# Block inverse read along rows, and padded loads, in a chunked recurrence on one Trainium2 core

## The chip, the core and the metric

The kernel runs on one core of a Trainium2 chip. The engines are named as the profile names them: PE multiplies matrices (PEld loads its weights), DVE works on vectors, ACT is the scalar engine, POOL is GpSimd, and SP issues most of the DMA transfers. Each engine takes its own instructions in order. The metric is the time of one execution in microseconds, the median over runs. Three runs of the kernel before gave 1887.94, 1891.57 and 1893.30 us.

## The reference

Per batch (4) and head (8) a 40 x 40 state is carried over 768 steps; then all outputs go through a mixture of 8 experts whose gate is normalized in rows and columns.

```python
for t in range(S):
    y[:, :, t] = np.einsum('bhd,bhde->bhe', rt, state)
    Sa = np.einsum('bhde,bhe->bhd', state, at)
    state_decay = state * wt[:, :, None, :] - np.einsum('bhd,bhe->bhde', Sa, bt)
    state = state_decay + np.einsum('bhd,bhe->bhde', vt, kt)
# x: the outputs, (3072, 320)
P = np.exp(x @ w_gate - max)       # then 8 rounds of row and column normalization
for e in range(E):
    out += P[:, e:e + 1] * (np.maximum(x @ w1[e], 0.0) @ w2[e])
```

## The kernel before, in words

The 768 steps are cut into 12 chunks of 64. Within a chunk the recurrence becomes matrix products and one triangular system per head, whose inverse is formed explicitly. Four steps `b` (the batches) stand for each chunk `c`; four pairs of heads lie side by side in a tile.

`prep(c, b)` loads the inputs (`inp`, 522 KB), scans the decays on DVE (`q`, `g`), forms `kb` and `ab` on POOL, and multiplies to the triangular matrices `ll`, whose lower part goes out to DRAM (`ld`). Two chunks form a group; there are six groups. When a group's eight preparations are out, `load_lu` brings their 32 x 32 blocks back as `lu`, one small matrix a partition (128 partitions: 2 chunks, 2 blocks, 4 batches, 8 heads), by eight DMAs.

The inverse of all 128 blocks then runs on DVE alone, in `un`. `inv_diag` (steps 1 to 7) inverts the 8 x 8 diagonal blocks, column by column. `inv_off` fills the blocks beside the diagonal, first 8 x 8, then 16 x 16, each by two products of small matrices. Such a product is a `contract`: one multiplication that spreads all products into `pr` and one reduction over the innermost index. The second factor `m` is a block of `lu` or `un` read down its columns:

```python
in1=m.rearrange("u k r -> u r k").unsqueeze(1).broadcast_to([nu, n_c, n_r, n_k])
```

A row is 32 floats, so neighbours in a column lie 128 bytes apart. The largest product has 2048 terms a partition. `finish` transposes the whole inverse (1024 elements, into `tn`, which shares the memory of `pr`) and stores both forms to DRAM (`ud`, `nd`). `tload` loads them back in other layouts (`td`, `tt`), and `tmat` joins 32 x 32 blocks to 64 x 64 with two PE products (`gp`, `op`).

`recur(c, b)` is the recurrence itself. It loads `vz` (value rows into columns 0 to 63 of a 104-wide tile; the state `z` goes to columns 64 to 103 by two ACT copies at the end of the step before), `rb`, and the transposed values into `f`, and then alternates between engines: `av` (PE), `f` (DVE), `xc` (PE), `x`, `c` (ACT), `pu` (PE, with `tt`), `pm` (DVE), `c` (PE), `ws` (DVE), `y`, `z` (POOL), `zt` (PE), `vz` (ACT). Four of these chains are in flight, one per batch.

The list `ev` holds all calls with a time each, sorted; a scheduler then sets the order on every engine from that list and its own estimates. The order in the built program is what each engine follows. The last part of the kernel, the experts (lines 545 to 687), begins as soon as the first outputs are there and is not touched.

## Time and profile before

| | |
|---|---|
| Median of 3 runs | 1891.57 us |
| Profiled execution | 1888.5 us, span 1886.7 us, granted PE clock 0.945 |
| Busy over the span: PE, DVE, ACT, POOL | 1768.5, 1395.1, 853.9, 896.9 us |
| First 118 us: PE, DVE, POOL busy | 53.0, 83.9, 71.4 us |
| 118 to 560 us: PE, DVE, POOL busy | 403.5, 322.4, 216.1 us |
| DMA busy share in slices 1 to 12 of 40, tenths | 8 5 6 7 7 7 7 8 5 5 7 3 |

The profile is of one execution by the hardware profiler. Busy times count overlapping work on different engines twice, so they do not add up to the span. The chain of work that ended last is followed backwards from the last instruction through whatever released each step; only time on it shortens the run directly. The first 560 us hold the recurrence, the rest is the experts, during which PE is busy nearly all the time.

### The profile page before, as it was taken

Reading aid. Unit: us, or ns where it says so; the run is one execution under the profiler, and the core shown is the slowest. Engines: PE = TensorE matmul, PEld = TensorE weight load, DVE = VectorE, ACT = ScalarE, POOL = GpSimd, SP = SyncE. Lnnn points to the kernel's source line nnn. Section 1 sums busy time; section 2 is a strip of 40 time slices with the busy share of each in tenths; the row PEclk is TensorE's granted clock in tenths of the full one; section 3 lists DMA queues with packets and bytes.
Section 4 is the critical chain, followed back from the end, with each engine's and each line's share of the span. In section 5 each row is a group of like instructions: output and inputs, shape, how many; then the busy total and the mean of one; then the engine's idle time right before and its main releaser. Section 6 shows DMA issues by size and latency. Waiting matters only on the chain.

```text
span 1886.7 us, 31821 instructions
## 1 busy us (share of the span) xinstructions
PE 1768.5 (94%) x12035; PEld 1731.1 (92%) x12035; DVE 1395.1 (74%) x2330; ACT 853.9 (45%) x1845; POOL 896.9 (48%) x845
## 2 busy tenths in 40 slices
PE   4478989889998999999999999999999999999999
PEld 4368878789888999999999999999999999999999
DVE  7766768686579877776867777886776767777676
ACT  6346566655553444343433434345343433434342
POOL 6636457562345355371835628004461826537170
PEclk9568889988889999999999999999999999999999
DMA  8567777855732011110201102111110201111011
GB/s 192 102 131 160 137 156 144 176 128 102 164 96 70 32 43 37 37 61 14 73 26 49 55 19 74 55 33 38 37 55 19 73 19 56 37 37 57 17 37 42
DMA packets 187838, 136.26 MB, mean 72 GB/s; under 512 B 155941, under 2 KB 165285, under 8 KB 187685
## 3 DMA queue, kind: packets, MB, share of 16 engines
q1 hardware_dynamic: 184485, 128.98, 27.6%
q10 hardware_dynamic: 3200, 5.25, 1.1%
q8 instruction: 95, 1.56, 0.3%
q14 instruction: 58, 0.48, 0.1%
HBM read 113.74 MB, written 20.45 MB: 71 GB/s over the span
## 4 chain that ended last, share of the span: by engine, by line
PE 76%; DVE 10%; DMA 6%; issue 3%; POOL 2%; ACT 2%; SPq 1%; DVEq 0%; POOLq 0%; ACTq 0%
PE op L610 35%; PE p L545 32%; DMA inp<-in_inp_dram 2%; PE xc L259 2%; DVE pr L179 2%; PE pu L270 1%; PE av L251 1%; PE c L277 1%; DVE q L114 1%; PE ll L145 1%; PE lp L307 1%; PE gp L226 1%; DMA nd<-pr 1%; POOL ab L140 1%; DVE g L122 1%
## 5 line engine op out<-in xcount | busy, mean ns | idle before, releaser
L545 PE MATMUL p<-xch,wh 128*128 128x384 f32 (+1 forms) x1792 | 605.3, 339 | 5.2 <-DVE cs L654 1.8
L566 ACT ACTIVATE hh<-sm 128x384 fp32r<-128x384 f32 x512 | 269.5, 527 | 726.3 <-DVE sm L563 726.3
L610 PE MATMUL op<-wh,hh 128*128 128x320 f32 x1536 | 477.3, 311 | 1.0 <-ACT hh L566 0.9
L610 PE MATMUL op<-wl,hh 128*128 128x320 f32 x1536 | 474.7, 310 | 0.0
L610 PE MATMUL op<-wh,hl 128*128 128x320 f32 x1536 | 468.0, 310 | 4.4 <-DVE hl L569 4.4
L491 POOL TENSOR_TENSOR wl<-ws,wh 128x640 fp32r<-128x640 f32 x60 | 103.1, 1719 | 608.4 <-ACT wh L489 608.1
L569 DVE SCALAR_TENSOR_TENSOR hl<-sm,hh 128x384 fp32r<-128x384 f32 x512 | 370.8, 757 | 2.8 <-ACT hh L566 2.3
L545 PEld LDWEIGHTS p<-xch,wh 128*128 128x128 f32 (+1 forms) x1792 | 337.9, 189 | 8.4 <-DVE u L563 2.7
L545 PE MATMUL p<-xcl,wh 128*128 128x384 f32 x896 | 303.1, 338 | 0.0
L545 PE MATMUL p<-xch,wl 128*128 128x384 f32 x896 | 302.3, 337 | 0.0
L610 PEld LDWEIGHTS op<-wh,hh 128*128 128x128 f32 x1536 | 290.6, 189 | 1.7 <-ACT hh L566 1.5
L610 PEld LDWEIGHTS op<-wh,hl 128*128 128x128 f32 x1536 | 287.1, 188 | 5.4 <-DVE hl L569 5.3
L610 PEld LDWEIGHTS op<-wl,hh 128*128 128x128 f32 x1536 | 291.4, 190 | 0.0
L563 DVE TENSOR_TENSOR sm<-p,u 128x384 f32<-128x384 f32 x384 | 232.6, 615 | 9.2 <-PE p L545 0.4
L545 PEld LDWEIGHTS p<-xcl,wh 128*128 128x128 f32 x896 | 169.0, 189 | 0.0
L545 PEld LDWEIGHTS p<-xch,wl 128*128 128x128 f32 x896 | 169.0, 189 | 0.0
L563 DVE TENSOR_TENSOR sm<-p,p 128x384 f32<-128x384 f32 x128 | 71.3, 557 | 130.1 <-PE p L545 76.2
L563 DVE TENSOR_TENSOR p<-p,p 128x384 f32<-128x384 f32 x128 | 71.1, 555 | 101.5 <-PE p L545 101.0
L563 DVE TENSOR_TENSOR u<-p,p 128x384 f32<-128x384 f32 x128 | 70.8, 553 | 59.4 <-PE p L545 58.1
L145 PE MATMUL ll<-ab,kb 104*128 104x128 f32 x336 | 61.3, 340 | 50.6 <-POOL ab L140 22.2
L499 POOL TENSOR_TENSOR wl<-ss,wh 128x512 fp32r<-128x512 f32 x60 | 90.7, 1512 | 32.1 <-ACT wh L496 28.0
L145 PEld LDWEIGHTS ll<-ab,kb 104*128 104x128 f32 x336 | 53.2, 241 | 54.7 <-POOL ab L140 27.4
(161 smaller groups left out, 2845.0 us busy)
## 6 DMA issues: line engine op xcount, KB each, us to landing
ws<-in_wts_dram SPq DMA_DIRECT2D x60, 832.0 KB
inp<-in_inp_dram SPq DMA_DIRECT2D x42, 521.6 KB
rb<-in_r_dram SPq DMA_DIRECT2D x48, 208.0 KB
ld<-lt ACTq DMA_DIRECT2D x40, 128.0 KB
vz<-in_v_dram SPq DMA_DIRECT2D x48, 104.0 KB
f<-in_vt_dram SPq DMA_DIRECT2D x48, 80.0 KB
xd<-y SPq DMA_DIRECT2D x96, 40.0 KB
st<-in_inp_dram SPq DMA_DIRECT2D x6, 521.6 KB
```

What stands on the lines that cost most here:

```text
L114: nc.vector.tensor_tensor_scan(out=q.rearrange("r p t -> r (p t)"), data0=w65[:, 0:260], data1=one65, initial=0.0, op0=ALU.mult, op1=ALU.add)
L122: nc.vector.tensor_tensor_scan(out=g.rearrange("r p t -> r (p t)"), data0=w65[:, 260:516], data1=g1.rearrange("r p t -> r (p t)"), initial ...
L145: nc.tensor.matmul(ll[:, p], lhsT=kb[:, p], rhs=ab[:, p], start=True, stop=True)
L179: nc.vector.tensor_tensor(out=prv, in0=a.unsqueeze(2).broadcast_to([nu, n_c, n_r, n_k]), in1=m.rearrange("u k r -> u r k").unsqueeze(1).br ...
L259: nc.tensor.matmul(xc[h][:, p], lhsT=pp["sx"][:, p, h], rhs=f[:, p, h], start=True, stop=True)
L491: g.tensor_tensor(out=wl[:, 0:640], in0=raw[:, 256:896], in1=wh[:, 0:640], op=ALU.subtract)
L499: g.tensor_tensor(out=lv[:, 3:7], in0=so[:, :, 0], in1=hv[:, 3:7, 0], op=ALU.subtract)
L545: nc.tensor.matmul(o, lhsT=w_, rhs=x_, start=(j == 0), stop=(j == 3))
L563: eng.tensor_tensor(out=out, in0=x, in1=y, op=ALU.add)
L566: nc.scalar.activation(out=hh[:, f, h], in_=sm[f][:, h], func=AF.Relu)
L569: v.scalar_tensor_tensor(out=hl[:, f, h], in0=sm[f][:, h], scalar=0.0, in1=hh[:, f, h], op0=ALU.max, op1=ALU.subtract)
L610: nc.tensor.matmul(ops[i], lhsT=a[:, h, cs], rhs=w_[:, cw], start=(f == 0 and h == 0 and j == 0), stop=(last and h == 1 and j == 2))
```

## The change

The second factor of every contraction is now read along rows, from a transposed copy. `flip_l` writes the transposes of the blocks of `lu` that are needed into `lu`'s unused lower half, once a group, before the first elimination step. `flip_d` and `flip_h` write transposes of the finished diagonal blocks of `un` into a tile `tn` of its own. `inv_off` is replaced by `inv_8` and `inv_16`, in which no product has more than 1024 terms: the two of 2048 become two each. `finish` transposes only the last 16 x 16 block, the others being in `tn` already.

Apart from that, the host pads the value rows to the full 104 columns with zeros and the transposed values to 104 columns a head, so that both are loaded in one contiguous piece a partition (104 pieces of 1664 bytes instead of 416 of 256; 64 of 3328 instead of 512 of 160). Because the load of `vz` now overwrites the columns of `z`, it is issued one chunk ahead, in the step that precedes its use, and the first four are issued before any preparation. `vz` is no longer cleared at the start; `tn` is, on POOL.

```diff
-    prf = inv.tile([128, 2048], F32, name="pr")
+    prf = inv.tile([128, 1024], F32, name="pr")
+    tnf = inv.tile([128, 1056], F32, name="tn")
...
+        nc.gpsimd.memset(tnf, 0.0)
-        for t in vz_b + c1_b + lg_b:
+        for t in c1_b + lg_b:
...
     def contract(us, dst, a, m):
-        n_c, n_r, n_k = a.shape[1], m.shape[2], a.shape[2]
+        n_c, n_r, n_k = a.shape[1], m.shape[1], a.shape[2]
-            in1=m.rearrange("u k r -> u r k").unsqueeze(1).broadcast_to([nu, n_c, n_r, n_k]), op=ALU.mult)
+            in1=m.unsqueeze(1).broadcast_to([nu, n_c, n_r, n_k]), op=ALU.mult)
...
+    def flip_l(us):
+        lh = half_t(luf, us)
+        nc.vector.tensor_copy(out=lh[:, :, 8:16, 0:8], in_=lh[:, :, 0:8, 8:16].rearrange("u b k r -> u b r k"))
+        nc.vector.tensor_copy(out=lu[us, 16:32, 0:16], in_=lu[us, 0:16, 16:32].rearrange("u k r -> u r k"))
+    def flip_d(us):
+        nc.vector.tensor_copy(out=tnd[us, :, 0:8, 0:8], in_=und[us, :, 0:8, 0:8].rearrange("u b c j -> u b j c"))
+    def flip_h(us):
+        nc.vector.tensor_copy(out=half_t(tnf, us)[:, :, 8:16, 0:8],
+                              in_=half_t(unf, us)[:, :, 0:8, 8:16].rearrange("u b c j -> u b j c"))
...
+    def inv_8(us, i):
+        o, g, un_ = 16 * i, gt(us, 8), un[us]
+        contract(us, g, un_[:, o:o + 8, o:o + 8], lu[us, o + 8:o + 16, o:o + 8])
+        contract(us, un_[:, o:o + 8, o + 8:o + 16], g, tn[us, o + 8:o + 16, o + 8:o + 16])
+    def inv_16(us, i):
+        g, un_, tn_, l16 = gt(us, 16), un[us], tn[us], lu[us, 16:32, 0:16]
+        if i == 0:
+            contract(us, g[:, 0:8, 0:8], un_[:, 0:8, 0:16], l16[:, 0:8])
+            contract(us, g[:, 0:8, 8:16], un_[:, 0:8, 0:16], l16[:, 8:16])
+        elif i == 1:
+            contract(us, g[:, 8:16], un_[:, 8:16, 8:16], l16[:, :, 8:16])
+            contract(us, un_[:, 0:16, 16:24], g[:, :, 0:8], tn_[:, 16:24, 16:24])
+        else:
+            contract(us, un_[:, 0:8, 24:32], g[:, 0:8], tn_[:, 24:32, 16:32])
+            contract(us, un_[:, 8:16, 24:32], g[:, 8:16], tn_[:, 24:32, 16:32])
-    INV = [(inv_diag, (i,)) for i in range(1, 8)] + [(inv_off, a) for a in ((0, 8, 8), (16, 8, 8), (0, 16, 8))]
+    INV = [(flip_l, ())] + [(inv_diag, (i,)) for i in range(1, 8)] + [(flip_d, ())]
+    INV += [(inv_8, (0,)), (inv_8, (1,)), (flip_h, ()), (inv_16, (0,)), (inv_16, (1,)), (inv_16, (2,))]
...
     def recur(c, b):
-        nc.sync.dma_start(out=vz[:, :, 0:64], in_=d["v"][c, b])
+        if c + 1 < NCH:
+            vn = rot("vz", vz_b)
+            nc.sync.dma_start(out=vn, in_=d["v"][c + 1, b])
...
-        nc.sync.dma_start(out=f[0:64].rearrange("s p h x -> s (p h) x")[:, :, 64:104],
-                          in_=d["vt"][c, b].rearrange("s (g x) -> s g x", x=40))
+        nc.sync.dma_start(out=f[0:64].rearrange("s p h x -> s (p h x)"), in_=d["vt"][c, b])
...
-        vz = rot("vz", vz_b)
+        vz = vn
...
+    for b in range(NB):
+        nc.sync.dma_start(out=vz_cur[b], in_=d["v"][0, b])
...
     def finish(s, us):
-        nc.vector.tensor_copy(out=tn[us], in_=un[us].rearrange("u c s -> u s c"))
+        nc.vector.tensor_copy(out=tn[us, 16:32, 0:16], in_=un[us, 0:16, 16:32].rearrange("u c j -> u j c"))
```

The instructions' order moves with it. Lines of the changed kernel are 6 to 30 higher; 120, 128 and 161 are what 114, 122 and 155 were (scans `q`, `g` and the masked triangle), 185 and 188 are the contraction's multiplication and reduction (179 and 182 before). In the rows below a tile's number is its buffer.

DVE at the start, the preparations of the first group. Before, the first step of the recurrence (`f`) stands behind the fourth preparation:

```order
L114 SCALAR_TENSOR_TENSOR q<-st_189,cst 104x260
L118 RECIPROCAL g_196<-q 104x4
L122 SCALAR_TENSOR_TENSOR g_163<-st_189,g_196 104x256
L155 TENSOR_TENSOR sx_153<-ll,cst 64x8x64
L139 TENSOR_TENSOR ab_195<-st_189,g_163 40x4x64
L140 TENSOR_TENSOR ab_195<-st_189,g_163 40x4x64
L252 TENSOR_TENSOR f<-av,cst 104x8x64
L114 SCALAR_TENSOR_TENSOR q<-inp,cst 104x260
L118 RECIPROCAL g_196<-q 104x4
```
Now it stands behind the fifth:

```order
L120 SCALAR_TENSOR_TENSOR q<-inp,cst 104x260
L124 RECIPROCAL g_196<-q 104x4
L128 SCALAR_TENSOR_TENSOR g_167<-inp,g_196 104x256
L161 TENSOR_TENSOR sx_157<-ll,cst 64x8x64
L145 TENSOR_TENSOR ab_194<-inp,g_167 40x4x64
L146 TENSOR_TENSOR ab_194<-inp,g_167 40x4x64
L280 TENSOR_TENSOR f<-av,cst 104x8x64
L120 SCALAR_TENSOR_TENSOR q<-inp,cst 104x260
L124 RECIPROCAL g_196<-q 104x4
```
One preparation has moved ahead of `f`, which waits for `av`.

DVE at the end of the first group's inverse, from the last but one product to the finishing copy, before:

```order
L122 SCALAR_TENSOR_TENSOR st_146<-inp,g_196 104x256
L179 TENSOR_TENSOR pr<-gt,un 128x1024
L155 TENSOR_TENSOR st_189<-ll,cst 64x8x64
L182 TENSOR_REDUCE un<-pr 128x16x8
L114 SCALAR_TENSOR_TENSOR q<-inp,cst 104x260
L179 TENSOR_TENSOR pr<-gt,un 128x2048
L118 RECIPROCAL g_196<-q 104x4
L155 TENSOR_TENSOR st_146<-ll,cst 64x8x64
L182 TENSOR_REDUCE un<-pr 128x16x8
L122 SCALAR_TENSOR_TENSOR st_147<-inp,g_196 104x256
L114 SCALAR_TENSOR_TENSOR q<-inp,cst 104x260
```
and now:

```order
L124 RECIPROCAL g_196<-q 104x4
L185 TENSOR_TENSOR pr<-gt,tn 128x1024
L128 SCALAR_TENSOR_TENSOR st_147<-inp,g_196 104x256
L161 TENSOR_TENSOR st_146<-ll,cst 64x8x64
L188 TENSOR_REDUCE un<-pr 128x8x8
L120 SCALAR_TENSOR_TENSOR q<-inp,cst 104x260
L185 TENSOR_TENSOR pr<-gt,tn 128x1024
L124 RECIPROCAL g_196<-q 104x4
L188 TENSOR_REDUCE un<-pr 128x8x8
L128 SCALAR_TENSOR_TENSOR st_148<-inp,g_196 104x256
L161 TENSOR_TENSOR st_147<-ll,cst 64x8x64
```
The product of 2048 has become two of 1024 with a reduction of its own each, scans and triangles of the next preparations stand between them, and the finishing copy has shrunk.

DVE behind the third group's finishing copy, before:

```order
L331 COPY pr<-un 128x1024
L252 TENSOR_TENSOR f<-av,cst 104x8x64
L118 RECIPROCAL g_196<-q 104x4
L279 TENSOR_TENSOR ws<-c_2466,c_202 104x416
L272 TENSOR_TENSOR pm<-pu,cst 128x416
L122 SCALAR_TENSOR_TENSOR st_146<-inp,g_196 104x256
L155 TENSOR_TENSOR st_189<-ll,cst 64x8x64
L252 TENSOR_TENSOR f<-av,cst 104x8x64
L279 TENSOR_TENSOR ws<-c_2600,c_203 104x416
L155 TENSOR_TENSOR st_146<-ll,cst 64x8x64
L312 COPY lg<-lp 64x8 x2
```
and now:

```order
L361 COPY tn<-un 128x16x16
L192 COPY lu<-lu 128x2x8x8
L193 COPY lu<-lu 128x16x16
L176 TENSOR_TENSOR pr<-un,lu 128x4
L179 TENSOR_REDUCE un<-pr 128x4
L176 TENSOR_TENSOR pr<-un,lu 128x16
L179 TENSOR_REDUCE un<-pr 128x4x2
L176 TENSOR_TENSOR pr<-un,lu 128x36
L340 COPY lg<-lp 64x8
L179 TENSOR_REDUCE un<-pr 128x4x3
```
Before, the recurrence's `f`, `ws` and `pm` and the triangles followed, and the next group's first elimination step stood nineteen rows below the copy; now the flip of the next group's `lu` follows at once. On SP at the same place, from the loads of the first chunk's inverse on, before:

```order
L334 DMA nd<-pr 64x1024 x2
L213 DMA td<-ud 32x16x32 x2
L211 DMA td<-nd 32x16x32 x2
L217 DMA tt_190<-ud 32x16x32 x4
L285 DMA xd<-y 40x4x64 x2
L109 DMA inp<-in_inp_dram 104x1284 x2
L240 DMA rb<-in_r_dram 104x512
L242 DMA f<-in_vt_dram 64x8x40
L217 DMA tt_191<-ud 32x16x32
L285 DMA xd<-y 40x4x64 x2
L217 DMA tt_191<-ud 32x16x32 x3
L342 DMA lu<-ld 16x32x32 x4
```
and now:

```order
L363 DMA ud<-un 64x1024
L364 DMA nd<-tn 64x1024
L240 DMA td<-ud 32x16x32
L238 DMA td<-nd 32x16x32 x2
L240 DMA td<-ud 32x16x32
L244 DMA tt_190<-ud 32x16x32 x4
L372 DMA lu<-ld 16x32x32 x4
L244 DMA tt_191<-ud 32x16x32 x4
```
The last four loads of `lu` have moved from behind the second chunk's `tt` to ahead of it.

More of the change, by code (lines that the diff above doesn't have):

```diff
@@ L72, in attention, with half_t @@
     luf = inv.tile([128, 1056], F32, name="lu")
-    prf = inv.tile([128, 2048], F32, name="pr")
+    prf = inv.tile([128, 1024], F32, name="pr")
     gtf = inv.tile([128, 256], F32, name="gt")
-    un, lu, tn = (t[:, 0:1024].rearrange("u (a b) -> u a b", b=32) for t in (unf, luf, prf))
-    und, lud = (t.rearrange("u (b x) -> u b x", x=264)[:, :, 0:256].rearrange("u b (c j) -> u b c j", j=32)
-                for t in (unf, luf))
+    tnf = inv.tile([128, 1056], F32, name="tn")
+    un, lu, tn = (t[:, 0:1024].rearrange("u (a b) -> u a b", b=32) for t in (unf, luf, tnf))
+    und, lud, tnd = (t.rearrange("u (b x) -> u b x", x=264)[:, :, 0:256].rearrange("u b (c j) -> u b c j", j=32)
+                     for t in (unf, luf, tnf))
+    def half_t(t, us):
+        return t[us].rearrange("u (b x) -> u b x", x=528)[:, :, 0:512].rearrange("u b (c j) -> u b c j", j=32)
     for t in g1_b + ab_b:
@@ L180, in contract @@
             out=prv, in0=a.unsqueeze(2).broadcast_to([nu, n_c, n_r, n_k]),
-            in1=m.rearrange("u k r -> u r k").unsqueeze(1).broadcast_to([nu, n_c, n_r, n_k]), op=ALU.mult)
+            in1=m.unsqueeze(1).broadcast_to([nu, n_c, n_r, n_k]), op=ALU.mult)
         nc.vector.tensor_reduce(out=dst, in_=prv, op=ALU.add, axis=AX.X)
-    def inv_off(us, o, n, h):
-        gt = gtf[us, 0:n * n].rearrange("u (c r) -> u c r", r=n)
-        un_, lu_ = un[us], lu[us]
-        if h == n:
-            contract(us, gt, un_[:, o:o + n, o:o + n], lu_[:, o:o + n, o + n:o + 2 * n])
-            contract(us, un_[:, o:o + n, o + n:o + 2 * n], gt, un_[:, o + n:o + 2 * n, o + n:o + 2 * n])
-            return
-        contract(us, gt[:, 0:h], un_[:, o:o + h, o:o + n], lu_[:, o:o + n, o + n:o + 2 * n])
-        contract(us, gt[:, h:n], un_[:, o + h:o + n, o + h:o + n], lu_[:, o + h:o + n, o + n:o + 2 * n])
-        contract(us, un_[:, o:o + n, o + n:o + n + h], gt[:, :, 0:h], un_[:, o + n:o + n + h, o + n:o + n + h])
-        contract(us, un_[:, o:o + n, o + n + h:o + 2 * n], gt, un_[:, o + n:o + 2 * n, o + n + h:o + 2 * n])
@@ new lines, in flip_h, with gt @@
+    def flip_h(us):
+        nc.vector.tensor_copy(out=half_t(tnf, us)[:, :, 8:16, 0:8],
+                              in_=half_t(unf, us)[:, :, 0:8, 8:16].rearrange("u b c j -> u b j c"))
+    def gt(us, n):
+        return gtf[us, 0:n * n].rearrange("u (c r) -> u c r", r=n)
+    def inv_8(us, i):
+        o, g, un_ = 16 * i, gt(us, 8), un[us]
+        contract(us, g, un_[:, o:o + 8, o:o + 8], lu[us, o + 8:o + 16, o:o + 8])
+        contract(us, un_[:, o:o + 8, o + 8:o + 16], g, tn[us, o + 8:o + 16, o + 8:o + 16])
@@ L378, in attention @@
         for i, (fn, a) in enumerate(INV):
-            ev.append((t + INV_DT * i, fn, (us,) + a))
+            ev.append((t + INV_DT * 10 * i / len(INV), fn, (us,) + a))
         ev.append((t + INV_DT * 10 + 0.01, finish, (s, us)))
@@ L789, in _layout @@
     cst[:, 400::65] = 1.0
-    arrays = dict(inp=inp, r=rb.reshape(NCH, NB, R2, NP, 128), v=packed(g["v"]),
+    vp = np.zeros((NCH, NB, R2, NP, 104), np.float32)
+    vp[..., 0:64] = packed(g["v"])
+    vq = np.zeros((NCH, NB, C, NH, 104), np.float32)
+    vq[..., 64:] = vt.reshape(NCH, NB, C, NH, D)
+    vt = vq.reshape(NCH, NB, C, NH * 104)
+    arrays = dict(inp=inp, r=rb.reshape(NCH, NB, R2, NP, 128), v=vp,
                   vt=vt, wts=wts, gate=gate, cst=cst)
```

## The prediction

> **What bounds the kernel now.** I read the page first: the span, the busy rows and the chain of work that ended last.
>
> ```profile
> span 1886.7 us, 31821 instructions
> PE 1768.5 (94%) x12035; PEld 1731.1 (92%) x12035; DVE 1395.1 (74%) x2330; ACT 853.9 (45%) x1845; POOL 896.9 (48%) x845
> PE 76%; DVE 10%; DMA 6%; issue 3%; POOL 2%; ACT 2%; SPq 1%; DVEq 0%; POOLq 0%; ACTq 0%
> PE op L610 35%; PE p L545 32%; DMA inp<-in_inp_dram 2%; PE xc L259 2%; DVE pr L179 2%; PE pu L270 1%; PE av L251 1%; PE c L277 1%; DVE q L114 1%; PE ll L145 1%; PE lp L307 1%; PE gp L226 1%; DMA nd<-pr 1%; POOL ab L140 1%; DVE g L122 1%
> ```
>
> Two thirds of the chain is the expert layers' matmuls (lines 545 and 610), which the change does not touch. What it touches is the recurrence in front of them, and there DVE line 179, the multiplication of the block inverse, is the largest DVE entry. So the next view is the table of stages: 0 to 118 us (first preparations and first inverse, until the first `pu` can run), then the steady recurrence in two halves. Columns after the stretch are sum, PE, PEld, DVE, ACT, POOL busy, granted clock, DMA share, GB/s.
>
> ```profile
> 0.00:118.00 118.00, 52.95 (x285) 47.87 (x286) 83.86 (x128) 52.05 (x129) 71.40 (x88) 0.66 0.72 149
> 118.00:340.00 222.00, 200.07 (x1763) 186.47 (x1764) 174.41 (x268) 138.91 (x351) 126.07 (x130) 0.89 0.71 146
> 340.00:560.00 220.00, 203.42 (x1794) 190.38 (x1793) 148.01 (x233) 127.83 (x311) 90.07 (x102) 0.85 0.61 134
> ```
>
> In the first stage PE works 53 of 118 us: it waits for others, and DVE (84 us) is the busiest. In the steady stages PE idles only 222 - 200.1 + 220 - 203.4 = 38.5 us, with DVE at 79% and 67%. A gain on DVE can therefore be paid out almost fully in stage one, and later only out of those 38.5 us (and out of the granted clock, 0.85 to 0.89, if PE pauses less). The chain within each of the three stretches says how much of it is line 179:
>
> ```profile
> by line: issue 10.1%; DVE g L122 7.4%; POOL ab L139 7.2%; DVE pr L179 6.8%; DVE q L114 5.9%; DMA vz<-in_v_dram 5.5%; DMA inp<-in_inp_dram 5.1%; DMA st<-in_inp_dram 4.8%; POOL ab L140 4.5%; DMA ld<-lt 4.4%; DMA lu<-ld 4.2%; SPq L217 3.3%; DM
> by line: issue 10.7%; DMA inp<-in_inp_dram 5.8%; DVE pr L179 5.5%; PE xc L259 5.3%; PE ll L145 4.7%; DMA nd<-pr 4.2%; PE pu L270 3.7%; PE c L277 3.7%; DVE q L114 3.3%; POOL z L292 3.2%; PE av L251 3.1%; DVE gt L182 3.0%; DMA lu<-ld 2.8%; PO
> by line: issue 10.3%; PE xc L259 10.1%; DMA inp<-in_inp_dram 8.6%; PE pu L270 7.2%; PE av L251 6.5%; PE c L277 4.6%; PE gp L226 4.4%; DVE pr L179 4.1%; PE lp L307 3.7%; DMA rb<-in_r_dram 3.7%; DMA xs<-xd 3.6%; DMA nd<-pr 3.5%; PE op L231 2.
> ```
>
> That is 0.068 x 118 = 8.0, 0.055 x 222 = 12.2 and 0.041 x 220 = 9.0 us: 29 us of line 179 on the chain.
>
> **The contractions.** The groups of DVE instructions, shapes kept apart (busy us, mean ns), with the one multiplication in this stretch that reads two contiguous SBUF operands of 512 elements (line 133) and the transposing copy (line 331):
>
> ```profile
> L179 DVE TENSOR_TENSOR pr<-un,lu 128x2048 f32<-128x2048 f32 x6 | 22.6, 3773 | 0.1
> L179 DVE TENSOR_TENSOR pr<-gt,un 128x2048 f32<-128x2048 f32 x6 | 22.3, 3723 | 0.0
> L179 DVE TENSOR_TENSOR pr<-gt,un 128x512 f32<-128x512 f32 x12 | 12.8, 1064 | 0.1
> L179 DVE TENSOR_TENSOR pr<-un,lu 128x512 f32<-128x512 f32 x12 | 12.4, 1037 | 0.1
> L179 DVE TENSOR_TENSOR pr<-gt,un 128x1024 f32<-128x1024 f32 x6 | 11.5, 1922 | 0.0
> L179 DVE TENSOR_TENSOR pr<-un,lu 128x1024 f32<-128x1024 f32 x6 | 11.5, 1918 | 0.0
> L182 DVE TENSOR_REDUCE gt<-pr 128x128 f32<-128x2048 f32 x6 | 13.7, 2283 | 0.0
> L182 DVE TENSOR_REDUCE gt<-pr 128x64 f32<-128x512 f32 x12 | 8.1, 674 | 0.1
> L182 DVE TENSOR_REDUCE gt<-pr 128x128 f32<-128x1024 f32 x6 | 7.2, 1202 | 0.0
> L133 DVE TENSOR_TENSOR st<-st,q 104x512 f32<-104x512 f32 x1 | 0.7, 661 | 0.0
> L331 DVE COPY pr<-un 128x1024 f32<-128x1024 f32 x6 | 6.4, 1071 | 0.0
> ```
>
> The multiplications cost 93.1 us in all and about 1.8 ns an element, where the reductions of the same products cost 1.15 ns. What sets them apart is that `in1` is read down a column, one float every 128 bytes; line 133, which reads along its rows, does 512 elements in 661 ns against 1037 to 1064. So I price a multiplication that reads rows like a reduction of its size: 0.67 us at 512 elements, 1.20 us at 1024. After the change each of the six groups has four of 512 and six of 1024 (the two of 2048 are halved): 24 x 0.67 + 36 x 1.20 = 59.4 us, a saving of 33.7 us, 36%. If the column is not the reason, it stays at 24 x 1.05 + 36 x 1.92 = 94.3 us: the bounds are -33.7 and +1.2 us, and I take the first, by line 133. Reductions go from 2 x (13.7 + 8.1 + 7.2) = 58.0 to the same 59.4 us, +1.4.
>
> [...]
>
> **The transposed copies.** Four new copies a group (128, 256, 256 and 128 elements), and the last transposition shrinks from 1024 to 256. By line 331's ns per element plus a small fixed part I estimate 0.2, 0.3, 0.3, 0.2 and 0.3 us: 1.3 us against 1.07, x 6 = +1.4 us, all of it inside the inverse. Its bounds are 0 and twice that. Five memsets of `vz` leave DVE at the start, in the shadow of the first load.
>
> **What POOL gains.** Two pairs of rows of the timeline, then four pieces of the chain, then POOL's line 140 over the run (min/median/max ns):
>
> ```profile
> 74.68 3.64 DVE L179 TENSOR_TENSOR pr<-un,lu 128x2048 f32<-128x2048 f32 x1
> 74.83 3.56 POOL L138 COPY st<-q 104x4 f32<-104x4 f32 x1 [0.80 <-DVE q L114]
> 305.07 3.71 DVE L179 TENSOR_TENSOR pr<-un,lu 128x2048 f32<-128x2048 f32 x1
> 304.92 4.46 POOL L140 TENSOR_TENSOR ab<-inp,g 40x256 f32<-40x256 f32 x1
> 81.93 2.82 POOL ab L139
> 153.87 3.16 POOL z L292
> 304.92 4.47 POOL ab L140
> 315.53 3.58 POOL z L292
> L140 POOL TENSOR_TENSOR ab<-inp,st x21: 721/727/5013, 49.7 to 425.7; 40x256 f32<-40x256 f32 x21
> ```
>
> A four-element copy on POOL lasts 3.56 us because it stands still while DVE's long multiplication runs; a 0.73 us product lasts 4.46. On the chain the four long POOL pieces make 14.0 us where 4 x 0.73 = 2.9 would do: 11.1 us of standing still. The longest block falls from 3.7 to 1.2 us, so up to two thirds of it could go; since other two-operand DVE work blocks too, I take half, -5.5 us.
>
> **What of that reaches the end.** On the chain: multiplications 36% of 29.2 = -10.6, reductions +0.5 (the same third of them as of the multiplications), copies +1.4, POOL -5.5: -14.2 us. Stage one holds -2.9 and about -1.0 of it and pays in full, since PE is idle there more than half the time: -3.9. The other -10.3 fall in stages where PE is busy 90% and where PE's own pieces (xc, pu, av) take the chain over when DVE's shorten; I count half, -5.2. Together -9.
>
> **The loads.** v goes from 416 pieces of 256 bytes to 104 of 1664, the transposed values from 512 pieces of 160 bytes to 64 of 3328: 760 pieces fewer and 198 KB more in each of 48 steps.
>
> ```profile
> DMA packets 187838, 136.26 MB, mean 72 GB/s; under 512 B 155941, under 2 KB 165285, under 8 KB 187685
> q1 hardware_dynamic: 184485, 128.98, 27.6%
> ```
>
> The 184,485 packets of the large queue took 27.6% of 16 engines, 521 us of the full set. If time goes by pieces, 36,500 fewer save 103 us of it; if it goes by bytes, at the stages' 146 GB/s for a share of 0.71 (206 GB/s for a full set), 9.5 MB more cost 46 us. DMA `inp` pieces are 6.0, 12.9 and 18.9 us of the three chains, 38 us; scaled by -27% or +12% (103 or 46 of the 377 us that DMA is busy before 560, by the table of stages) that is -10 or +5 us at the end. Stretches with small and with large pieces both move close to 200 GB/s when full, so I take 0. In SyncE's queue each step's two issues get shorter at most; nothing is moved behind a new wait, since the load of the next `vz` stands where the old one stood, beside `rb`, and waits for an `av` that `rb`'s buffer also waits for: 0.
>
> [...]
>
> **The start.** Four `vz` loads of 173 KB now stand ahead of the first `inp`.
>
> ```profile
> 5.00:10.00 5.00, 0.96 (x4) 0.64 (x4) 3.68 (x7) 2.92 (x9) 4.76 (x11) 1.00 0.87 211
> 7.43 0.70 DVE L114 TENSOR_TENSOR_SCAN q<-st,cst 104x260 f32<-104x260 f32 x1 [1.06 <-DMA st<-in_inp_dram]
> 24.08 0.69 DVE L252 TENSOR_TENSOR f<-av,cst 104x512 f32<-104x512 f32 x1 [2.22 <-PE av L251]
> ```
>
> 0.69 MB at 211 GB/s delay the first scan from 7.4 to 10.7 us. Against that, the fifth preparation now stands ahead of `f` on DVE, where DVE waited 2.2 us: +1 us net, bounds 0 and +3.3.
>
> **The boundary of two groups.** In one place the order changes for the worse: after the third inverse DVE goes straight on to flip the next group's `lu`, while before nineteen rows of the recurrence stood between.
>
> ```profile
> 337.51 1.02 DVE L331 COPY pr<-un 128x1024 f32<-128x1024 f32 x1
> 338.56 1.08 SPq L334 DMA_DIRECT2D nd<-pr  x2
> 353.04 0.56 DVE L272 TENSOR_TENSOR pm<-pu,cst 128x416 f32<-128x416 f32 x1
> 356.98 2.02 SPq L342 DMA_DIRECT2D lu<-ld  x4
> 362.43 0.17 DVE L170 TENSOR_TENSOR pr<-un,lu 128x4 f32<-128x4 f32 x1 [3.22 <-DMA lu<-ld]
> ```
>
> Before, `lu` landed 24 us after the finishing copy, and the next `pm` ran 15 us after it. In the new order SyncE issues `lu` ahead of the second half's `tt`, about 10 us after the copy (14 issues of 0.5 us, by the `lu` row, and one landing), so it may land some 15 us after it, and the queued `pm` then follows the first elimination steps, at about 19: up to +5 us. The same move ends the fourth inverse two steps of the recurrence earlier, which I let pay it back: 0, bounds -3 and +15.
>
> **The sum.** -9 + 1 = -8 us. The profiled execution took 1888.5 us (span 1886.7), 3 us under the median of the three runs, 1891.6; the sum applies to both. From the median that gives 1883.6, from the profiled one 1880.5; I say 1882.
>
> **Rivals.**
> First, DVE is the true bound of the recurrence and everything on its chain is paid out: -14.2 and more, because a granted clock of 0.85 rises when PE pauses less (1% of 440 us is 4 us): about -20, 1872. For it: DVE at 79%; against it: PE at 90%.
> Second, fewer pieces make every landing shorter: the -10 of the loads on top, 1874.
> Third, slower: DVE's wait at the flip for `lu`. It decides if `lu` lands more than about 20 us after the copy, as it did before (24); then `pm`, `f` and `ws` of the running chunk stand behind it in DVE's queue, +15 us, and with the -8 of the rest the end is +7: 1899.
> Fourth, it does not do what it says: a multiplication costs its count whatever it reads; +1.2 +1.4 +1.4 on DVE, a third on the chain, and +1 at the start: 1893.
> Fifth, PE is the bound after 118 us and only stage one pays: -3.9 + 1, 1888.7.
>
> **Chances.** My forecast 0.42 (its own range 1875 to 1888), first rival 0.22, second 0.08, third 0.15, fourth 0.04, fifth 0.09. A difference of 0.3%, 5.7 us, is about what the runs can tell from none. Faster: 0.37 of the forecast's 0.42, with 0.22 and 0.08: 0.67. Slower: the third rival but for a little, 0.14. The rest, 0.19, is the same. The range 1862 to 1898 reaches over the first two rivals' spread below and to the third's near edge above.
>
> **What would show it.** Multiplications at 1.2 us for 1024 elements and 0.67 for 512, no POOL product above about 2.5 us, the first `pu` some 3 us earlier than 118, PE's idle time between there and 560 us smaller by about 5. Wrong if multiplications stay near 1.9 us for 1024 (fourth rival), if DVE shows a wait above 10 us for `lu` at a flip (third), or if `inp` pieces on the chain change much in either direction (second).

## The result, and the profile after

The changed kernel takes 1914.59 us (median of 4 runs, 1913.05 to 1918.09) against 1889.76 before (1883.56 to 1893.30): a ratio of 1.0128, 95% interval 1.0099 to 1.0157. It is slower by 1.3%, where the prediction said faster: 1882 us, with a range from 1862 to 1898. The profiled execution took 1915.66 us.

The page first: the span, the busy row and the shares of the DMA queue. DVE is 33 us less busy than before and POOL 31, packets are 36,500 fewer, bytes 9.5 MB more; PE, which has the same 12035 matmuls to do, is 21 us busier.

```profile
span 1913.9 us, 31872 instructions
PE 1789.9 (94%) x12035; PEld 1746.3 (91%) x12035; DVE 1361.9 (71%) x2373; ACT 855.6 (45%) x1845; POOL 866.2 (45%) x846
DMA packets 151359, 145.76 MB, mean 76 GB/s; under 512 B 111397, under 2 KB 125733, under 8 KB 151205
q1 hardware_dynamic: 148005, 138.47, 28.4%
```

The table of stages, the same three as before (the stretch and its sum, busy time of PE, PEld, DVE, ACT, POOL, then granted clock, DMA share, GB/s). In the first, PE has done 6 us more; in the third the clock is 0.77, where it was 0.85.

```profile
0.00:118.00 118.00, 58.99 (x317) 53.06 (x317) 78.83 (x141) 54.81 (x134) 62.50 (x89) 0.67 0.73 160
118.00:340.00 222.00, 193.34 (x1730) 179.56 (x1729) 157.66 (x278) 138.35 (x349) 109.52 (x129) 0.87 0.77 165
340.00:560.00 220.00, 201.40 (x1570) 185.01 (x1570) 129.79 (x234) 116.40 (x286) 81.10 (x97) 0.77 0.65 151
```

More telling is a stretch that holds the same work in both: from the first `pu` of the recurrence to the last (48 steps of four pairs). First before, then after, the same columns:

```profile
118.00:555.00 437.00, 398.49 (x3514) 371.99 (x3514) 319.02 (x492) 265.37 (x659) 214.68 (x229) 0.87 0.67 142
```

```profile
113.00:581.00 468.00, 420.74 (x3519) 388.96 (x3519) 295.64 (x535) 265.91 (x660) 194.28 (x231) 0.82 0.68 151
```

The changed kernel starts 5 us earlier and takes 31 us longer: that is the result. PE idles 468 - 420.7 = 47.3 us instead of 38.5 (+8.8), and it is busy 22.2 us longer with the same 3,515 or so matmuls, because its granted clock is 0.82 instead of 0.87. From the last `pu` to the end both take 1332 to 1333 us.

The starts of single `pu` steps say where: steps 0, 8, 15, 16, 24, 32, 39, 47 are at 118, 194, 259, 272, 351, 435, 487, 555 us before, and at 113, 181, 248, 275, 352, 434, 505, 581 after. A lead of 11 to 13 us is lost at once between steps 15 and 16, another 18 us between 32 and 39, and 8 more by the last step.

At the first place, DVE, then PE, in the timeline (start, duration, engine and line; in brackets the wait and what ended it). DVE does stand 13.85 us in front of the flip for `lu`. But `pm`, which is queued behind, waits for a `pu` that PE starts only at 274.88, since PE itself waits 11 us for `td`, the third inverse's way back from DRAM: the recurrence has run dry.

```profile
261.77 0.35 DVE L361 COPY tn<-un 128x256 f32<-128x256 f32 x1
275.97 0.27 DVE L192 COPY lu<-lu 128x128 f32<-128x128 f32 x1 [13.85 <-DMA lu<-ld]
279.46 0.58 DVE L300 TENSOR_TENSOR pm<-pu,cst 128x416 f32<-128x416 f32 x1
```

```profile
269.39 1.88 PE L253 MATMUL gp<-td,lg 64*64 64x32 f32 x16 [11.03 <-DMA td<-nd]
274.88 2.04 PE L298 MATMUL pu<-x,tt 128*128 128x104 f32 x8
```

Around that pause the clock is at half for 34 us (the windows of 1 us show it below 0.75 from 257 to 291). It fell some 2 us before the pause began, behind one of 1.7 us, and was still at half 21 us after PE had resumed. At the second place it is at half from 458 to 489 us behind a pause of 2.5; there PE is busy all the time and does 115 matmuls in 20 us:

```profile
460.00:480.00 20.00, 20.00 (x115) 18.51 (x114) 11.06 (x16) 7.87 (x20) 3.19 (x4) 0.50 0.22 60
```

### The profile page after: what moved, and what is told of

Read it like the earlier page. It is cut to its first block, busy times and chain, and to the rows that moved or that the text cites. A ratio compares the mean times of both kernels' runs of the same rounds, so it can differ in the third digit from the quotient of the medians.

```text
span 1913.9 us, 31872 instructions
## 1 busy us (share of the span) xinstructions
PE 1789.9 (94%) x12035; PEld 1746.3 (91%) x12035; DVE 1361.9 (71%) x2373; ACT 855.6 (45%) x1845; POOL 866.2 (45%) x846
## 3 DMA queue, kind: packets, MB, share of 16 engines
q1 hardware_dynamic: 148005, 138.47, 28.4%
## 4 chain that ended last, share of the span: by engine, by line
PE 73%; DVE 5%; DMA 2%; issue 1%; ACT 1%; SPq 0%; POOL 0%; DVEq 0%; ACTq 0%; POOLq 0%
PE op L640 34%; PE p L575 32%; PE xc L287 2%; PE av L279 1%; PE c L305 1%; PE pu L298 1%; PE lp L335 1%; DMA inp<-in_inp_dram 1%; DVE hl L599 1%; DVE sm L593 1%; PE op L258 0%; PE gp L253 0%; DMA xs<-xd 0%; PE zt L325 0%; DVE u L593 0%
## 5 line engine op out<-in xcount | busy, mean ns | idle before, releaser
L151 PEld LDWEIGHTS ll<-ab,kb 104*128 104x128 f32 x336 | 54.6, 247 | 48.5 <-POOL ab L146 27.6
```

Of the source, the lines that this page charges most:

```text
L151: nc.tensor.matmul(ll[:, p], lhsT=kb[:, p], rhs=ab[:, p], start=True, stop=True)
```

## The experiments

Each ratio is against runs of the kernel before on the same chip. "Half" is the sum of the windows of 1 us between 110 and 600 us whose granted clock is below 0.75; "idle" is PE's, between the first and the last `pu` of the profiled execution.

| kernel | ratio, 95% interval | first pu, us | to last pu, us | idle, us | half, us |
|---|---|---|---|---|---|
| before | 1 | 118 | 437 | 38.5 | 131 |
| changed | 1.0128 [1.0099, 1.0157] | 113 | 468 | 47.3 | 174 |
| inv_only | 1.0023 [0.9988, 1.0058] | 112 | 446 | 29.3 | 147 |
| load_only | 1.0243 [1.0187, 1.0299] | 122 | 472 | 58.4 | 164 |
| f_only | 1.0128 [1.0093, 1.0164] | 122 | 450 | 38.4 | 164 |
| v_only | 1.0158 [1.0108, 1.0208] | 123 | 453 | 52.3 | 142 |
| ballast | 1.0082 [1.0049, 1.0115] | 124 | 448 | 42.2 | 153 |
| fence_last | 1.0104 [1.0062, 1.0145] | 115 | 466 | 44.8 | 178 |
| fence_all | 1.0242 [1.0202, 1.0282] | 114 | 486 | 59.9 | 202 |

The ratios are of several executions; the last four columns are of the one that was profiled and show a kernel only roughly. f_dep (below), whose time can't be told from before, has 156 us at half in its profiled execution, which took 12 us more than its median; v_only's took 12 us less than its median and fence_last's 7 more. The mean granted clock of a whole execution is on record for all of them: 13 of the kernel before, run beside inv_only, average 0.945, ten of inv_only 0.941 and four of load_only 0.930. Those 13 alone range from 1879.68 us at 0.953 to 1897.65 us at 0.939, so the time of one and the same kernel goes with its clock.

**One part of the change alone, and the order (first four).** From the traces my first theory (A) was the order on DVE: the flip right behind the third finish, and the sixth inverse drawn together ahead of `f` and `ws`. Theory B blames the loads, theory C the inverse itself. inv_only is the changed kernel with the old loads; the main lines of its edit are

```diff
-        if c + 1 < NCH:
-            vn = rot("vz", vz_b)
-            nc.sync.dma_start(out=vn, in_=d["v"][c + 1, b])
+        nc.sync.dma_start(out=vz[:, :, 0:64], in_=d["v"][c, b])
...
-        nc.sync.dma_start(out=f[0:64].rearrange("s p h x -> s (p h x)"), in_=d["vt"][c, b])
+        nc.sync.dma_start(out=f[0:64].rearrange("s p h x -> s (p h) x")[:, :, 64:104],
+                          in_=d["vt"][c, b].rearrange("s (g x) -> s g x", x=40))
...
```

> The row-reading inverse alone, with the loads of the kernel before. On DVE the pieces of groups 2, 3 and 5 (counted from 0) stand between the same steps of the recurrence as before (group 5 from the 33rd pm to the 40th), only group 4 is drawn together (24th to 27th pm). Theory A (the order of the inverse on DVE costs the 25 us: the wait for lu behind the third finish, and the sixth inverse drawn together ahead of f and ws): about 1882 us, 1874 to 1890, since neither place is there, with up to 6 us for group 4. Theory B (the padded and earlier loads cost it): 1875 to 1885 as well. Theory C (the inverse itself, its copies and additional instructions, costs it): 1905 to 1915. Tells C from the others.

Measured: 1893.93 us, 1.0023. C falls; so does the forecast of the inverse's gain, since A and B both said 1890 at most. load_only is the kernel before with the same lines the other way round:

> The padded loads, with vz a chunk ahead, alone; the old inverse. The pieces of the inverse stand between nearly the same steps as before. Theory A: 1887 to 1895, near before, with the start 2 to 3 us later. Theory B: 1905 to 1916, with inp pieces larger on the chain. Theory C: 1887 to 1895.

Measured: 1930.45 us, 1.0243. The loads cost 2.4% on their own; with the inverse, 1.3%. So the two parts do not simply add: with the old loads no gain of the inverse shows, and with the padded ones it takes back about 1.1% (1.0243 against 1.0128, intervals apart). Why was not tried. The same stretch from first to last `pu`, of inv_only, then of load_only:

```profile
112.00:558.00 446.00, 416.70 (x3521) 385.48 (x3521) 298.93 (x535) 265.72 (x660) 190.73 (x231) 0.84 0.67 140
```

```profile
122.00:594.00 472.00, 413.57 (x3513) 382.94 (x3511) 323.20 (x494) 265.66 (x659) 230.29 (x233) 0.84 0.67 150
```

In these executions the inverse takes 9.2 us of PE's idle time away (29.3 for 38.5) and 6 us ahead of the first `pu`, and gives it back: PE is busy 18.2 us longer, at a clock of 0.84 instead of 0.87. The loads add 19.9 us of idle time and 15.1 of busy time. fence_last and fence_all hold pieces of the inverse in the changed kernel back with tiny copies, which read a `pm` of the recurrence and so must wait for it (fence_last in the sixth group, fence_all in the third to the sixth):

```diff
+    def fence(us, n, l=False):
+        pm = pms.pop(n)
+        nc.vector.tensor_copy(out=prf[us, 0:1], in_=pm[us, 0, 0:1])
+        if l:
+            nc.vector.tensor_copy(out=luf[us, 256:993:736], in_=pm[us, 0, 0:2])
...
```

> The changed kernel whole, with six tiny DVE copies in the sixth group's inverse, each of one element of a pm tile: they hold its pieces back so that they stand between the 33rd and 39th pm, as in the kernel before, instead of most of them ahead of the 34th. The place behind the third group's finish is left as it is. Theory A: the stretch from step 32 to step 47 of the recurrence falls from 147 us to about 125 (before: 120), and the time from 1914.6 to 1890 to 1897; PE's granted clock between 460 and 480 us rises from 0.50 to above 0.8. Theories B and C: 1912 to 1918, since no load and no product is changed.

Measured: 1906.61 us, between what the theories gave. Steps 32 to 47 took 131 us, and the clock between 460 and 480 us rose as theory A said:

```profile
460.00:480.00 20.00, 20.00 (x160) 18.57 (x159) 10.73 (x21) 9.12 (x24) 2.47 (x5) 0.80 0.40 98
```

But step 32 was reached at 449 us instead of 434, though the inverses up to there stand as in the changed kernel; half time moved instead of going away (178 for 174).

> The same tiny copies in groups 2 to 5, so that every one of these inverses starts behind the same pm as before and is spread like before (17th, 25th, 33rd to 22nd, 30th, 39th; the second from the 10th). Theory A: both losses vanish and the lead of 11 to 13 us at step 15 stays: 1880 us, 1873 to 1888. Theory B: no lower than 1905. Theory C: no lower than 1905, more if the order that was left helps.

Measured: 1933.31 us. With every inverse where the kernel before has it, the changed kernel is slower still. Theory A falls, and with inv_only and load_only theory B, the loads, stands. (The copies cost something themselves, see inv_fence_all below, so 1933 is not the price of that order alone.)

**The loads in parts.** In the kernel before, f_only pads the transposed values alone and v_only the value rows alone, with their early issue and the four loads at the start; ballast adds dead bytes:

```diff
+        nc.sync.dma_start(out=dead, in_=d["wts"][0, 0, :, 0:336])
...
```

> The kernel before with the transposed values alone padded: f is loaded in 64 pieces of 3328 bytes (208 KB, 128 more a step), so its load now also writes the columns that DVE's f writes. Theory B1 (the bytes cost it: 198 KB more a step lost about 39 us when both loads were padded): 128/198 of that, +25, 1912 to 1920. Theory B2 (the new dependence: DVE's f, which stands in DVE's order, must wait until the load has landed): most of the 39, 1915 to 1930, with DVE waiting for f's load. Theory B3 (the early issue of vz and its four loads ahead of the first inp): 1888 to 1896.

> The kernel before with the value rows alone padded and loaded a chunk ahead: 65 KB more a step, four loads at the start. B1: 65/198 of 39, +13, 1900 to 1907. B2: +3, the start, 1890 to 1896. B3: most of the 39, 1915 to 1930.

> The kernel before, and in each step of the recurrence one more load of 172 KB in 128 pieces of 1344 bytes behind f's, into a tile that nobody reads: bytes alone, and the order on DVE as before. B1: 172/198 of 39, +34, 1920 to 1930. B2 and B3: 1888 to 1898.

Measured: 1912.77, 1920.41 and 1904.09 us. What DVE's scan `q` waits for `inp` between 118 and 560 us (us in total, times, longest), in the kernel before, the changed one, f_only, v_only, ballast:

```profile
DVE q L114 <- DMA inp<-in_inp_dram: 20.5, 15, 3.3
```

```profile
DVE q L120 <- DMA inp<-in_inp_dram: 39.4, 17, 7.0
```

```profile
DVE q L114 <- DMA inp<-in_inp_dram: 40.9, 14, 7.2
```

```profile
DVE q L114 <- DMA inp<-in_inp_dram: 14.8, 9, 2.7
```

```profile
DVE q L115 <- DMA inp<-in_inp_dram: 29.0, 12, 4.8
```

Padded `f` doubles the wait, dead bytes raise it by less than half, early `vz` doesn't raise it. Each is one execution, and f_dep, which loads next to nothing more, shows 25.4 us, so only the doubling stands clear. 172 KB a step that nobody reads cost 0.8%, about 15 us, which is less than theory B1 (bytes alone) and more than the others forecast. By that rate the 128 KB more of padded `f` would be some 11 of its 24 us, and for `vz` bytes are the smaller part (65 KB, some 6 us of 30). The next ones split the rest. f_dep keeps `f`'s bytes nearly as before and adds the new dependence, that DVE's `f` must wait for the load (in columns 63 to 103):

```diff
-        nc.sync.dma_start(out=f[0:64].rearrange("s p h x -> s (p h) x")[:, :, 64:104],
-                          in_=d["vt"][c, b].rearrange("s (g x) -> s g x", x=40))
+        nc.sync.dma_start(out=f[0:64].rearrange("s p h x -> s (p h) x")[:, :, 63:104],
+                          in_=d["vt"][c, b].rearrange("s (g x) -> s g x", x=41))
...
```

> The kernel before, but the transposed values are loaded as 41 columns a head, into columns 63 to 103 of f: column 63 is also written by DVE's f, so that f now has to wait for the load as in the changed kernel, at nearly the same bytes (82 KB for 80) and pieces. The order on every engine is that of the kernel before. Theory B2 (the new dependence is what padded f cost beside its bytes: 24 us measured, some 11 of them bytes by the 15 us that 172 dead KB cost): 1899 to 1905. Theory B1 (bytes and their collisions alone): 1886 to 1893.

Measured: 1889.23 us, 1.0008 [0.9980, 1.0036]. The dependence costs nothing that shows: B2 falls, and the bytes are what is left. Why they cost more in `f`'s load than as dead bytes is open. v_early, v_early_ns and v_nostart move the value rows' issue (the first two unpadded, and in the last two the first four loads stand behind the first six `inp`; in v_early the clearing of `vz` now follows the first four loads, so that its first chunk sees zero values and DVE's clearing waits for them):

> The kernel before, with the value rows not padded (416 pieces of 256 bytes, 104 KB) but issued a chunk ahead, the first four ahead of the first inp. Theory S (the earlier issue and the start cost what padded value rows cost, 18 to 31 us): 1905 to 1920. Theory B1 (their 65 KB more a step): 1889 to 1897, the start's 2 to 4 us aside.

> Padded value rows issued a chunk ahead, but the first four behind the first six inp instead of ahead of them. If the start is the matter (first pu at 123 instead of 118 us, then a lasting shift): 5 us less than v_only, 1905 to 1915, first pu at 118. If not: as v_only, 1910 to 1925.

> Value rows not padded, issued a chunk ahead, the first four behind the first six inp; nothing else of the change. If the early issue in SyncE's queue costs time in the steady part (it moves rb and f behind a wait for the av of the step just before): 1900 to 1912. If the start is all of it (v_early gave 1927 with the four loads first): 1886 to 1893.

Measured: v_early 1926.70 us, 1.0199 [1.0130, 1.0268]; v_nostart 1906.01, 1.0092 [1.0064, 1.0120]; v_early_ns 1899.23, 1.0071 [1.0047, 1.0094]. Of the 1.6% of v_only the issue a chunk ahead is 0.7%, which needs no additional byte, and the four loads ahead of the first `inp` about as much (v_only against v_nostart; the intervals overlap a little, and v_early against v_early_ns gives 1.3%, with the clearing in it). The padding adds little (v_nostart against v_early_ns, overlapping).

How an issue's place can cost ten microseconds is to be read where the lead is lost. SyncE's queue in the changed kernel, and then in inv_only, around the second finish:

```profile
159.99 2.22 SPq L363 DMA_DIRECT2D ud<-un  x2
162.30 1.87 SPq L364 DMA_DIRECT2D nd<-tn  x2
...
169.05 2.08 SPq L244 DMA_DIRECT2D tt<-ud  x4
171.51 0.69 SPq L313 DMA_DIRECT2D xd<-y  x2
172.24 0.38 SPq L115 DMA_DIRECT2D inp<-in_inp_dram  x1
```

```profile
160.70 0.52 SPq L115 DMA_DIRECT2D inp<-in_inp_dram  x1
...
161.86 0.50 SPq L360 DMA_DIRECT2D ud<-un  x1
163.19 0.49 SPq L361 DMA_DIRECT2D nd<-tn  x1
```

The last `inp` of the third group stands behind the finished inverse's stores and loads in the one and ahead of them in the other. It is issued 11.5 us later, the third group's first elimination step comes at 210.3 instead of 192.6 us, its finishing copy at 261.8 instead of 244.7, and step 16 of the recurrence at 275 instead of 258. In the kernel before the last three came at 207.6, 259.5 and 272 us, so what goes here is the lead of the new inverse. This chain is read off single traces; no run changed that place alone.

**The inverse with the old loads in other orders.** inv_fence_all and inv_fence4 have the copies in the third to the sixth group or in the fifth, inv_fence4s three of them; inv_use makes `lu`'s transposes right before their use.

> The row-reading inverse with the old loads, and six tiny DVE copies that hold the fifth inverse's pieces back, between the 25th and the 31st pm, where the kernel before has them (without them all stand between the 24th and 27th). Theory: that place cost inv_only 14 us (its steps 24 to 32 took 90 us, with 35 us on end at half clock, against 84; its lead of 14 us at step 16 was gone by 32): 1880 us, 1874 to 1886, and the half-clock time between 110 and 600 us falls from 147 to some 115. Rival (the clock's half time follows from PE's packing, not from this place): another pause opens another half-clock stretch, 1888 to 1898.

> The row-reading inverse with the old loads and the tiny DVE copies in groups 2 to 5, so that each inverse starts and ends behind the same pm as in the kernel before. With the padded loads the same copies gave 1933 us. Theory L (the loads cost what the changed kernel loses; the inverse's place matters little): 1882 to 1892. Theory F (it is the copies and the spread place that made 1933): above 1905.

> The row-reading inverse with the old loads, and lu's transposed copies made right before their use instead of ahead of the first elimination step. Of the inverse's groups only the fifth (25th to 30th pm) stands otherwise than in inv_only, spread instead of drawn together. If the inverse is worth its 9 us wherever it is not drawn together: 1878 to 1886. If its gain on idle time is given back as half clock in any order: 1887 to 1897.

> As inv_fence4 with three tiny copies instead of six (fifth inverse between the 25th and the 30th pm). inv_fence4 gave 0.998 of the time before. Same two cases: 1878 to 1886, or 1887 to 1897.

Measured: inv_fence4 1886.62 us, 0.9982 [0.9956, 1.0007]; inv_fence_all 1901.74, 1.0095 [1.0060, 1.0130]; inv_use 1883.68, 0.9980 [0.9949, 1.0011]; inv_fence4s 1892.29, 1.0015 [0.9975, 1.0055]. The five orders of the same inverse reach from 0.2% faster to 1% slower, none clearly faster than before; half time is 142 to 166 us in their profiled executions, 131 before. inv_use came out in its first case and inv_fence4s in its second; inv_fence4 kept 152 us of half clock where 115 had been expected, and inv_fence_all came between its two cases. With the same copies the padded loads cost 1.5% (fence_all against inv_fence_all). No version here is shown to beat the kernel before.

**The clock.** pause and mix are kernels of plain blocks of matmuls, with pauses of PE between them.

> Nothing of the reference is computed: blocks of 220 fp32 matmuls of 104 x 104 weights by 128 columns, and between two blocks PE waits for DVE operations of 64, 512, 1024, 1536, 2048, 3072, 4096, 6144 and 8192 columns, some 1 to 9 us. Clock theory: a pause above about 2 us is followed by a stretch of half clock (matmuls of 0.54 us instead of 0.27) that lasts 7 us or more, longer than the pause itself; pauses below 1.5 us leave the clock at 1. Rival (the clock falls for reasons of the kernel's mix, not of the pause): the clock stays at 1 or recovers within 4 us whatever the pause.

The windows behind idle times of 2.41, 2.94 and 4.01 us (stretch, PE and PEld and DVE and POOL busy, clock):

```profile
302.00:305.00 3.00, 3.00 (x15) 3.00 (x16) 0.00 (x0) 0.00 (x0) 0.50 0.02 5
306.00:351.00 45.00, 45.00 (x415) 45.00 (x414) 0.00 (x0) 0.00 (x0) 1.00 0.00 1
355.00:402.00 47.00, 47.00 (x433) 47.00 (x432) 0.00 (x0) 0.00 (x0) 1.00 0.00 1
407.00:411.00 4.00, 4.00 (x22) 4.00 (x23) 0.00 (x0) 0.00 (x0) 0.59 0.02 4
412.00:456.00 44.00, 44.00 (x405) 44.00 (x404) 0.00 (x0) 0.00 (x0) 1.00 0.01 1
```

Pauses up to 1.9 us left the clock at 1, one of 2.4 halved it and one of 2.9 did not; and the clock was back 3.5 us after the end of the pause of 2.4 and 4.1 us after that of 4.0. So in these plain blocks a pause alone did not make 34 us at half: the rival was right in that.

> Nothing of the reference is computed: nine blocks of fp32 matmuls, each behind a pause of PE of some 5 us, which halves the clock: 1 av alone; 2 av, xc, pu, c with changing weights; 3 the same with lp, gp and transposes between; 4 gp alone; 5 lp alone; 6 transposes alone; 7 as 2 with zeros; 8 eight xc and a short wait for DVE, again and again; 9 sixteen xc and a wait. Theory G (gaps between small groups keep the clock at half): blocks 1 to 3 recover within 4 us, block 8 (and 9) stays at half for 10 us and more. Theory K (small matmuls do): blocks 4, 5 or 3 stay at half. Rival: all recover within 4 us, and the long half-clock stretches of the recurrence, 7 to 35 us, come from something that these blocks don't hold.

Windows of mix: large matmuls behind a pause, at first and then; the mixed block behind its first run of small ones; 64 x 64 weights by 32 columns (as `gp`); 104 x 64 by 8 (as `lp`); transposes; eight large ones and a wait of 0.27 us, repeated; sixteen and a wait of 0.52 us, at first and later:

```profile
67.00:71.00 4.00, 3.88 (x18) 3.88 (x19) 0.26 (x3) 0.00 (x0) 0.50 0.00 0
72.00:116.00 44.00, 44.00 (x447) 44.00 (x446) 0.00 (x0) 0.00 (x0) 1.00 0.01 1
136.00:139.00 3.00, 3.00 (x18) 3.00 (x17) 0.00 (x0) 0.00 (x0) 0.51 0.00 0
191.00:276.00 85.00, 84.67 (x794) 84.67 (x795) 0.47 (x4) 0.00 (x0) 0.50 0.00 1
282.00:367.00 85.00, 84.95 (x797) 84.95 (x797) 0.19 (x2) 0.00 (x0) 0.50 0.00 1
379.00:393.00 14.00, 14.00 (x160) 14.00 (x158) 0.00 (x0) 0.00 (x0) 1.00 0.01 1
454.00:534.00 80.00, 73.71 (x384) 67.81 (x382) 4.18 (x23) 0.00 (x0) 0.50 0.00 1
540.00:555.00 15.00, 13.96 (x79) 13.45 (x79) 0.85 (x2) 0.00 (x0) 0.50 0.00 0
557.00:590.00 33.00, 28.34 (x288) 26.82 (x287) 3.84 (x9) 0.00 (x0) 1.00 0.01 1
```

Both G (gaps) and K (small matmuls) hold in the blocks. Small matmuls kept the clock at half for as long as they lasted, with PE busy throughout (85 us each at 0.50, fourth and fifth row), and so did waits of 0.27 us every 3.4 us (80 us at 0.50); sixteen matmuls to a wait recovered after 16 us. Transposes alone did not keep it there (14 us at 1.00, sixth row). In the mixed block three of the four short runs of `lp`, `gp` and transposes between large ones are followed by 3.4 us at half (136 to 139 us in the third row, and twice more). lp_wide asks whether `lp` does it in the recurrence:

```diff
-        lp = pt.tile([64, E], F32, name="lp", tag="pt")
+        lp = pt.tile([64, 64], F32, name="lp", tag="pt")
```

> The kernel before, with the gate's matmuls (lp) padded with zero columns from 8 to 64: the same instructions in the same order, but none of 8 columns. In the block kernel matmuls of 8 and 32 columns kept the clock at half for as long as they lasted, and short groups of them among large ones halved it for 3.4 us. Theory K (lp's groups hold the clock down in the recurrence too): half-clock time between 110 and 600 us falls from 131 to below 110, and the time is 1878 to 1890 although PE has some 15 us more to do. Rival (it is the gaps between groups, which padding leaves): half-clock time stays at 125 to 150 and the time is 1893 to 1905.

Measured: 1929.53 us, 1.0204 [1.0144, 1.0265], which can't be read as it stands: the gate's wider weights were also put in another part of the memory, and between 560 and 640 us the experts' first product waits for its input as it doesn't before (wait in us, times, longest).

```profile
PEld p L545 <- ACT xch L519: 27.4, 1, 27.4
```

Before that, the last `pu` came at 565 us, 10 later than before, and half time up to 560 us was 127 against 125. In that one execution widening `lp` to 64 columns brought nothing: the recurrence's half clock isn't `lp`'s eight columns alone. Whether it is `gp` and `op`, or the short waits, was not tried.

## Why the prediction was wrong, step by step

**The contractions: right.** The groups of DVE in the changed kernel (busy us, mean ns), with the first copy and what it waited for:

```profile
L185 DVE TENSOR_TENSOR pr<-gt,tn 128x1024 f32<-128x1024 f32 x18 | 22.7, 1262 | 0.1
L185 DVE TENSOR_TENSOR pr<-un,lu 128x1024 f32<-128x1024 f32 x18 | 21.8, 1210 | 0.1
L185 DVE TENSOR_TENSOR pr<-un,lu 128x512 f32<-128x512 f32 x12 | 8.8, 735 | 0.1
L185 DVE TENSOR_TENSOR pr<-gt,tn 128x512 f32<-128x512 f32 x12 | 8.4, 697 | 0.2
L192 DVE COPY lu<-lu 128x128 f32<-128x128 f32 x6 | 1.6, 269 | 32.4 <-DMA lu<-ld 19.0 <-DMA tt<-ud 10.2 <-DMA xd<-y 3.3
```

The multiplications take 61.7 us against 59.4 forecast and 93.1 before; the five copies take 1.9 us a group where 1.3 was estimated. The fourth rival falls: for 1024 elements the rows read along show 1.21 and 1.26 us, the columns before 1.92.

**POOL: right, with one exception.** The group of `ab` products in which one took 5.0 us now has 1.77 us at most (2.05 is the longest of the other `ab` products), and POOL is 31 us less busy. One `kb` product still took 3.37 us, where the prediction said none above 2.5. It ran beside a scan `g` of 0.67 us and a multiplication of 1.19 us; undisturbed it takes 1.17. That scans hold POOL up too shows in the trace before: the four-element copy at 12.42 us took 0.59 us beside one, 0.18 at its shortest. What the 5.5 us that were put on the chain came to was not measured apart:

```profile
L146 POOL TENSOR_TENSOR ab<-inp,st x21: 720/727/1774, 52.0 to 424.7; 40x256 f32<-40x256 f32 x21
```

**What of that reaches the end: wrong.** The first stage paid more than the 3.9 us: the first `pu` came 5 us earlier with the loads' start in it, 6 in inv_only. In the later stages PE's idle time did fall by 9 us in inv_only. But the step took PE's busy time as given, and in the first rival it even let the clock rise. In inv_only the busy time grew by 18 us, as the clock in that stretch fell, with less idle time, from 0.87 to 0.84, and in that execution this is where the inverse's gain went. More executions agree in the sign: in all five orders of the inverse with the old loads the mean clock of a whole execution, averaged over 9 or 10, lies 0.004 to 0.013 below that of the kernel before beside them (13 to 18). Why the recurrence spends more time at half clock with the faster inverse is not settled; the blocks show two things that can do it.

**The loads: the step that failed most.** "so I take 0", bounds -10 to +5: measured alone, +2.4%, 40 us between the medians. Two parts of it were wrong. The bytes were weighed by the share of time that DMA is busy, which moved as little as I said (27.6% to 28.4%). But by the traces the price is paid where a transfer stands in front of an `inp` that DVE's queue waits for (40.9 us of such waits in f_only, 20.5 before), and dead bytes alone cost 15 us, three times my upper bound. And "nothing is moved behind a new wait": the early load waits for the `av` of the step just before, one step later than `rb`'s buffer does, and the scheduler arranged SyncE's queue anew around it. What the queue waits for `av` at `rb` in the kernel before, then at `vz` and at `rb` in the changed one (118 to 560 us; us in total, times, longest); at `vz` it did not wait for PE before:

```profile
SPq L240 <- PE av L251: 6.6, 6, 2.3
```

```profile
SPq L267 <- PE av L279: 23.2, 15, 4.2
SPq L269 <- PE av L279: 3.6, 2, 1.9
```

Not all of that is the new wait: in inv_only, with the old loads, `rb` waits 15.3 us for `av`. The early issue alone cost 0.7%. The second rival falls too: 36,500 packets fewer gained nothing that shows. What fewer pieces are worth at the same bytes was not measured, since the bytes grew as the pieces fell. Nor do full stretches all move close to 200 GB/s, as the step has it: in the trace before it is 213 at a share of 0.98 (20 to 30 us), 165 at 0.92 (280 to 300) and 143 at 0.86 (200 to 220).

**The start: right in its size, wrong in its weight.** The first scan moved from 7.4 to 10.0 us, close to the 10.7 forecast; but by v_only against v_nostart four loads ahead of the first `inp` cost 0.7% at the end, some 12 us (intervals overlapping a little).

**The boundary of two groups: right rows, wrong place, wrong cause.** The rows that I quoted of the trace before, from 337.5 us on, belong to the fourth finish, while the order showed the third. The wait that the third rival names appeared, 13.85 us, and would have been read as its proof. Yet `lu` was there 14 us after the copy, as the step had said (some 15) and within the 20 that the rival set; and `pm` behind it waited for `pu`, and PE for `td`: by the trace the third inverse was late because its last preparation was. The rival had the sign and not the mechanism. No rival had the loads making it slower.

## What to carry to other kernels

Price a load not by the queue's busy share but by what stands behind it in its queue and who waits there in order (load_only: a share of 0.67 from first to last `pu`, as before, and 40 us more); padding that saves pieces may cost more in bytes than it saves (f_only: 1.3% slower with 128 KB more a step), and a prefetch moves every later issue (0.7% for the early issue alone). Where PE is 90% busy in small pieces, look at its granted clock in the stretch before spending a gain on its idle time: idle time saved can come back as half clock (inv_only: 9 us less idle, 18 us more busy). Try the parts of a change apart, since of these two one alone cost 2.4% and the other nothing that shows, and the order in which a scheduler packs the same work was worth 1%.
